# Attention and two feed-forward layers on one core: the weight rounding split into four planned operations, and two thirds of the key sums added before the matrix product

## The chip, the cores and the metric

One core of a Trainium2 chip runs the whole program. The metric is device time in microseconds from launch to the end. TensorE is called PE below, its weight loads PEld, VectorE DVE, ScalarE ACT, GpSimd POOL; SP's queue issues the DMAs.

## The reference, cut to what matters

Attention with exponential features, then a feed-forward layer with a leaky unit, then four gated experts:

```python
def phi(x):                                   # x: (4, 8, 576, 64), w_phi: (64, 128)
    proj = np.einsum('bhsd,df->bhsf', x, w_phi)
    proj = proj - np.max(np.abs(proj), axis=-1, keepdims=True)
    return np.concatenate([np.exp(proj), np.exp(-proj)], axis=-1)
q_p, k_p = phi(q), phi(k)
kv = np.einsum('bhsf,bhsd->bhfd', k_p, v)
z = np.sum(k_p, axis=2)                       # the key sums
num = np.einsum('bhsf,bhfd->bhsd', q_p, kv)
den = np.einsum('bhsf,bhf->bhs', q_p, z)[..., None] + 1e-06
attn = num / den
...
h = x @ w_in                                  # x: (2304, 512), w_in: (512, 2048)
x = (np.maximum(h, 0) + alpha * np.minimum(h, 0)) @ w_out
...
out = sum(p[:, e:e+1] * (np.maximum(x @ w1[e], 0) @ w2[e]) for e in range(4))
```

## The kernel before, in words

**Attention** takes two heads at a time: 16 pairs, numbered 0 to 15. The 576 keys of a pair are five tiles (four of 128, one of 64), handled as three units: tiles 0 and 1, tiles 2 and 3, tile 4. For a unit, PE projects keys (`Pk`, lines 339 to 341, three fp32r products a tile) into a PSUM tile `bank`; DVE takes the largest magnitude (line 346) and subtracts it (line 353, into `pmk`); ACT takes the two exponentials (line 359, into `ke`, a ring of two buffers); PE multiplies with the values (`KV`, line 370, two heads in two column halves) and, with a block of ones as the stationary operand, adds the keys up (line 376, 32 columns wide, in four column groups). Both land in the PSUM tile `kv`, of which there is one. Two ACT copies bring it to SBUF (`kvs`), PE turns it (lines 390 and 392), ACT copies it to `kvt`. Queries are projected and reduced alike (`pmq`), transposed on PE (line 411), exponentiated on ACT (line 418, `qe`) and multiplied with `kvt` (line 428); ACT and DVE copy numerator and denominator out of PSUM; DVE inverts the denominator in four instructions (lines 440 to 443); POOL, ACT and DVE form the result and split it into two fp32r parts `Xh` and `Xl`.

**Beside it** run two kinds of work that do not belong to a pair. Eight float64 weight blocks of the first feed-forward layer are rounded to fp32: a DMA, one ACT instruction (line 529), four DVE instructions with integer and float operations in the function `words` (lines 185 to 188), an add (line 533, DVE or POOL), and the split into two fp32r parts. And products of that layer for the first three blocks of 512 tokens: `U` (line 222, 12 matmuls into `mm`, a ring of two PSUM tiles), its leaky unit on DVE and ACT (lines 556 to 561, tiles `t`, `gh`, `gl`), and `M` (line 243, four chunks of 12 matmuls, which needs `gh` and `gl` of all four `U`), which ACT copies to `acc_a`. That is 24 groups of 12 matmuls.

**The order** of all this is made by a planner in the kernel, the class `Plan`: each operation has a cost by engine, predecessors, a rank, ring buffers that it allocates and reads. The planner repeatedly takes the operation that can begin first (ties by rank), on the engine that suits it, and writes its instructions; every engine then executes its own in that order. An operation is never interrupted by another on the same engine. `words` is one operation of four instructions here.

**After attention** the rest of the first layer (chunks of weights rounded the same way by `rounded`, lines 190 to 195) and the expert layer (lines 794 and 841) follow, in an order that the framework makes.

Of the kernel before, what the change touches and what calls it, by code (L numbers as in the profile page):

```python
# [11 lines left out]
F32 = mybir.dt.float32  # L12
F32R = mybir.dt.float32r
U32 = mybir.dt.uint32
AF = mybir.ActivationFunctionType
ALU = mybir.AluOpType
# [3 lines left out]
P = 128  # L20
B, H, S, D, F = 4, 8, 576, 64, 128
NP = H // 2
NT = B * S
DM = H * D
CC = DM // P
DFF = 2048
E, DE = 4, 1024
# [3 lines left out]
BLK = 512  # L31
# [3 lines left out]
UNITS = [(0, 1), (2, 3), (4,)]  # L35
# [8 lines left out]
EP = NF2 // 2  # L44
SEQ = (1, 5, 6, 2, 7, 3, 4)
NA = 3
AHEAD = 2


RANK = dict(  # L50
    ld=6.41, sp=11.67, Pk=-7.81, Pq=-3.81, E=11.17, Z=-20.34, KV=-7.89, TV=-14.97, Q=-17.39, A=-0.59, F=2.88,
    W=22.69, U=16.42, G=5.73,
)
WSTEP = 0.46
# [4 lines left out]
class Plan:  # L59
# [11 lines left out]
    def op(self, name, costs, after, rank, emit, alloc=(), reads=(), behind=(), late=0):  # L71
        self.ops[name] = (costs, after, rank, emit, alloc, {*after, *behind}, late)
        for x in reads:
            self.readers.setdefault(x, []).append(name)
# [63 lines left out]
def fused(ctx: ExitStack, tc: tile.TileContext, qT, kT, v_main, v_tail, w_phi, alpha, probs, w64, wup, wdn, out):  # L138
    nc = tc.nc
    pool = lambda name, bufs, stack=ctx, **k: stack.enter_context(tc.tile_pool(name=name, bufs=bufs, **k))  # L140
    f32 = lambda ap: ap.bitcast(F32)
# [21 lines left out]
    acc = [big.tile([P, CC, NA * BLK], F32, name="acc_a")]  # L163
# [17 lines left out]
    wts = {}  # L181
    raw = {}

    def words(r, u, lo, hi):
        nc.vector.tensor_scalar(r, r, 3, None, ALU.logical_shift_left)
        nc.vector.scalar_tensor_tensor(r, hi, 1 << 31, r, ALU.bitwise_and, ALU.bitwise_or)  # L186
        nc.vector.tensor_scalar(u, r, 0xFF800000, None, ALU.bitwise_and)
        nc.vector.scalar_tensor_tensor(f32(u), lo, 2.0**-52, f32(u), ALU.mult, ALU.mult)

    def rounded(w, r, u):  # L190

# [76 lines left out]
    with ExitStack() as st1:  # L268
# [8 lines left out]
        for args in (  # L277
            ("kr", 1, F32, P, S), ("qr", 1, F32, P, S), ("v", 1, F32, P, len(TILES), 2, D),
            ("kh", 1, F32R, P, S), ("kl", 1, F32R, P, S), ("qh", 1, F32R, P, S), ("ql", 1, F32R, P, S),
            ("m", 13, F32, P, 4), ("pmk", 2, F32, P, 4, F), ("pmq", 3, F32, P, 4, F), ("ke", 2, F32, P, 4, 2, F),  # L280
            ("kvs", 1, F32, P, 4, F), ("qe", 4, F32, P, 2, HMAX), ("kvt", 4, F32, P, 4, P),
            ("den", 2, F32, P, S), ("dt", 1, F32, P, S), ("num", 2, F32, P, S), ("di", 3, F32, P, S // 32, 1),
            ("gh", 5, F32R, P, BLK), ("gl", 5, F32R, P, BLK), ("t", 2, F32, P, BLK),
        ):
            ring(*args)
        ring("bank", 5, F32, P, 512, space=PSUM)
# [1 line left out]
        ring("mm", 2, F32, P, BLK, space=PSUM)  # L288
        ones = pool("ones", 1, st1).tile([P, 32], F32, name="ones")
        one = const.tile([P, 1], F32, name="one")  # L290
        busy = pool("busy", 1, st1).tile([P, 2 * F], F32, name="busy")
        tl = {}

        def new(name, key, dtype=None):
            p_, shape, dt = rings[name]
            tl[name, key] = p_.tile(shape, dtype or dt, name=name)
            return tl[name, key]

        engines = {"a": nc.scalar, "v": nc.vector, "p": nc.gpsimd}
        pe = lambda n, k=1: k * (n / 2.4 + 3)  # L300
        act = lambda n: 100 + 0.83 * n
        actp = lambda n: 52 + 0.83 * n
        dve = lambda n: 70 + 1.04 * n
        dve2 = lambda n: 70 + 0.52 * n
# [4 lines left out]
        op = plan.op  # L309
# [53 lines left out]
        def key_values(p, u):  # L363

            unit = UNITS[u]
            rows, e, v = TILES[unit[0]][1], flat(tl["ke", (p, u)]), tl["v", p]
            kv = new("kv", p) if u == 0 else tl["kv", p]
            for i, tile_ in enumerate(unit):
                for h in range(2):
                    nc.tensor.matmul(  # L370
                        kv[h * D:(h + 1) * D, 0], v[:rows, tile_, h], e[:rows, 2 * i + h],
                        start=tile_ == 0, stop=tile_ == len(TILES) - 1, skip_group_check=True)
            for i, tile_ in enumerate(unit):
                for h in range(2):
                    r = 32 * (2 * (tile_ % 2) + h)
                    nc.tensor.matmul(  # L376
                        kv[r:r + 32, 1], ones[:rows], e[:rows, 2 * i + h],
                        start=False, stop=tile_ + 2 >= len(TILES), tile_position=(0, r), skip_group_check=True)

        def save_kv(p, k, e):  # L380
            kvs = (new if k == 0 else lambda *x: tl[x])("kvs", p).rearrange("p (k s) f -> p k (s f)", k=2)
# [75 lines left out]
        for p in range(len(pairs)):  # L457
# [16 lines left out]
                op(("E", p, u), {"a": 2 * act(N_U[u])}, [("S", "k", p, u)], RANK["E"] + p + 0.1 * u, alloc=[("ke", (p, u))],  # L474
                   reads=[("pmk", (p, u))], emit=lambda e, a=(p, u): exp_keys(*a))
            for u in range(3):
                op(("KV", p, u), {"t": 595 * len(UNITS[u])}, [("E", p, u), ("ld", "v", p)] + [("KV", p, u - 1)] * (u > 0),
                   RANK["KV"] + p + 0.1 * u, alloc=[("kv", p)] if u == 0 else [], reads=[("ke", (p, u)), ("v", p)],
                   emit=lambda e, a=(p, u): key_values(*a))
            for k in range(2):  # L480
                op(("CV", p, k), copy_cost(256), [("KV", p, 2)], RANK["TV"] + p, alloc=[("kvs", p)] if k == 0 else [],
                   behind=[("CV", p, 0)] * k, reads=[("kv", p)], emit=lambda e, a=(p, k): save_kv(*a, e))
            op(("TV", p), {"t": 340}, [("CV", p, 0), ("CV", p, 1)], RANK["TV"] + p, alloc=[("bank", ("kv", p)), ("kvt", p)],
               reads=[("kvs", p)], emit=lambda e, p=p: turn_kv(p))
# [37 lines left out]
        def w_step(i, k, e):  # L522
            c, half = early[i]
            st64, w, u = areas[i % 2]
            lo, hi = st64[:, :, 0::2], st64[:, :, 1::2]
            if k == 0:
                nc.sync.dma_start(st64, w64[c, half].rearrange("p (a b) -> p a b", a=2))
            elif k == 1:
                nc.scalar.mul(f32(w), f32(hi), 2.0**-112)
            elif k == 2:  # L530
                words(w, u, lo, hi)
            elif k == 3:
                engines[e].tensor_tensor(f32(w), f32(w), f32(u), ALU.add)
            elif k == 4:
                for r, n in ((wa[half], "h"), (wa[half], "l")):
                    tl["w" + n, (c, half)] = r.tile([P, DM], F32R, name="w" + n + "ud"[half])
                cp(engines[e], tl["wh", (c, half)].rearrange("p (a b) -> p a b", a=2), f32(w))
            else:
                h, l = (tl["w" + n, (c, half)].rearrange("p (a b) -> p a b", a=2) for n in "hl")
                engines[e].tensor_tensor(l, f32(w), f32(h), ALU.subtract)  # L540
                wts[c, half] = tl["wh", (c, half)], tl["wl", (c, half)]

        for i, (c, half) in enumerate(early):
            costs = ({"d": 1500}, {"a": act(DM)}, {"v": 2 * dve2(DM) + 2 * dve(DM) + 330}, lo_cost(DM), hi_cost(DM), lo_cost(DM))
            for k, cost in enumerate(costs):
                op(("W", k, c, half), cost, [("W", k - 1, c, half)] * (k > 0), RANK["W"] + WSTEP * i,
                   alloc=[("area", i)] * (k == 0), reads=[("area", i)] * (k == 5), late=4200 * (k == 0),
                   emit=lambda e, i=i, k=k: w_step(i, k, e))


        def g_step(c, blk, k, e):
# [381 lines left out]
```

## Time and profile before

| | us |
|---|---|
| median of three runs | 1405.55 (1403.22 to 1406.3) |
| the profiled execution, its own time | 1402.89 |
| its span | 1401.0 |
| PE busy | 1380.2 |
| DVE / ACT / POOL busy | 774.2 / 509.5 / 272.8 |

The span is what the profiler saw; 1.9 us lie around it. PE is busy for all but 20.8 us of it. Attention ends at about 279 us, where the products of the last pair end; the three early blocks of the first layer end at about 323 us.

### The profile page before, as it was taken

How to read it: one execution, taken by the hardware profiler on the slowest of the kernel's cores; microseconds unless marked ns; L12 is line 12 of the kernel's file. 1: busy time of each engine (PE TensorE's matmuls, PEld its weight loads, DVE VectorE, ACT ScalarE, POOL GpSimd, SP SyncE). 2: the span in 40 equal slices, each digit the busy share in tenths (PEclk: the TensorE clock that was granted, in tenths of full speed). 3: DMA queues.
4: the chain of work that ended last, by engine and by line, in shares of the span. 5: the costliest groups of instructions: out<-in, count | busy, mean ns of one | idle time of the engine just before them, and what ended most of it. 6: DMA issues, size and time to landing. Idle time of an engine off the chain costs nothing.

```text
span 1401.0 us, 19675 instructions
## 1 busy us (share of the span) xinstructions
PE 1380.2 (99%) x7304; PEld 1167.4 (83%) x7304; DVE 774.2 (55%) x1292; ACT 509.5 (36%) x1112; POOL 272.8 (19%) x276
## 2 busy tenths in 40 slices
PE   8999999989999999999999999999999999999998
PEld 5667766668888888889889898999899889988997
DVE  7876655587967956575544454633333363333343
ACT  6876666632212212124434443322122232221220
POOL 3443322221201104006655562000000000000000
PEclk9999999999999999999999999999999999999999
DMA  4311111032200202005886776665556667655541
GB/s 155 112 52 52 52 51 52 10 105 61 90 16 20 71 1 90 31 0 211 314 294 226 245 254 222 207 228 189 166 171 192 191 205 229 197 184 165 174 157 45
DMA packets 102208, 192.25 MB, mean 137 GB/s; under 512 B 11617, under 2 KB 12769, under 8 KB 102113
## 3 DMA queue, kind: packets, MB, share of 16 engines
q1 hardware_dynamic: 102112, 191.00, 42.2%
q8 instruction: 58, 0.95, 0.3%
q14 instruction: 38, 0.30, 0.1%
HBM read 140.10 MB, written 50.86 MB: 136 GB/s over the span
## 4 chain that ended last, share of the span: by engine, by line
PE 91%; DVE 4%; ACT 2%; DMA 2%; POOL 1%; issue 0%; SPq 0%; POOLq 0%; DVEq 0%
PE dn L841 28%; PE up L794 24%; PE up L222 12%; PE dn L243 12%; PE bank L428 4%; PE kv L370 2%; PE mm L243 2%; PE mm L222 2%; PE kv L376 2%; PE bank L411 1%; PE bank L339 1%; PE bank L341 1%; PE bank L340 1%; DMA acc_a<-w 0%; DVE acc_a L186 0%
## 5 line engine op out<-in xcount | busy, mean ns | idle before, releaser
L841 PE MATMUL dn<-whd,Xh 128*128 128x512 f32 x720 | 231.4, 390 | 0.0
L852 DVE SCALAR_TENSOR_TENSOR acc<-dn,pr,acc 128x512 f32<-128x512 f32 x126 | 88.7, 750 | 190.9 <-PE dn L841 190.9
L794 PE MATMUL up<-Xl,wlu 128*128 128x384 f32 x864 | 158.8, 335 | 1.0 <-DVE c L807 0.5
L841 PEld LDWEIGHTS dn<-whd,Xh 128*128 128x128 f32 x720 | 135.2, 188 | 27.0
L794 PEld LDWEIGHTS up<-Xl,wlu 128*128 128x128 f32 x864 | 150.3, 188 | 2.3 <-DVE c L807 1.4
L841 PE MATMUL dn<-Xh 128*128 128x512 f32 x648 | 151.8, 389 | 0.0
L807 DVE TENSOR_TENSOR c<-up,p 128x384 f32<-128x384 f32 x96 | 53.5, 558 | 174.7 <-PE up L794 172.0
L841 PEld LDWEIGHTS dn<-Xh 128*128 128x128 f32 x648 | 121.7, 188 | 25.5
L812 ACT COPY p<-up 128x384 f32<-128x384 f32 x48 | 23.0, 480 | 326.1 <-PE up L794 326.1
L841 PE MATMUL dn<-wld,Xh 128*128 128x512 f32 x360 | 140.8, 391 | 0.0
L794 PE MATMUL up<-Xl,whu 128*128 128x384 f32 x576 | 112.0, 334 | 0.8 <-ACT p L812 0.7
L801 ACT ACTIVATE Xh<-c 128x384 fp32r<-128x384 f32 x144 | 75.7, 526 | 79.3 <-DVE c L807 79.3
L794 PEld LDWEIGHTS up<-Xl,whu 128*128 128x128 f32 x576 | 101.2, 188 | 1.4 <-ACT p L812 1.4
L222 PE MATMUL up<-Xl,whu 128*128 128x512 f32 (+1 forms) x272 | 99.1, 364 | 0.0
L222 PE MATMUL up<-Xh,whu 128*128 128x512 f32 (+1 forms) x272 | 99.1, 364 | 0.0
L243 PE MATMUL dn<-gh,wld 128*128 128x512 f32 (+1 forms) x272 | 99.1, 364 | 0.0
L243 PE MATMUL dn<-gh,whd 128*128 128x512 f32 (+1 forms) x272 | 99.1, 364 | 0.0
L222 PE MATMUL up<-Xh,wlu 128*128 128x512 f32 (+1 forms) x272 | 99.0, 364 | 0.0
L243 PE MATMUL dn<-gl,whd 128*128 128x512 f32 (+1 forms) x272 | 99.0, 364 | 0.0
L175 ACT CAST gh<-t 128x512 fp32r<-128x512 f32 (+1 forms) x68 | 38.6, 568 | 149.5 <-DVE t L234 149.5
L802 DVE SCALAR_TENSOR_TENSOR Xh<-c,Xh 128x384 fp32r<-128x384 f32 x144 | 85.5, 595 | 5.5
L841 PEld LDWEIGHTS dn<-wld,Xh 128*128 128x128 f32 x360 | 67.5, 188 | 13.0
(166 smaller groups left out, 2481.7 us busy)
## 6 DMA issues: line engine op xcount, KB each, us to landing
whu<-wsu SPq DMA_DIRECT2D x96, 256.0 KB, 3.5
wlu<-wsu SPq DMA_DIRECT2D x96, 256.0 KB, 3.2
st<-w SPq DMA_DIRECT2D x24, 512.0 KB, 3.6
wsu<-whu SPq DMA_DIRECT2D x48, 256.0 KB, 3.1
wsu<-wlu SPq DMA_DIRECT2D x48, 256.0 KB, 2.6
Xh<-wsd SPq DMA_DIRECT2D x48, 256.0 KB, 3.8
wld<-wsd SPq DMA_DIRECT2D x40, 256.0 KB, 3.1
whd<-wsd SPq DMA_DIRECT2D x40, 256.0 KB, 3.6
```

The costliest lines, as they stand in the source:

```text
L175: nc.scalar.copy(hi, src)
L222: nc.tensor.matmul(ps[:, :bn], a[:, cs], x[:, cc, t0:t0 + bn], start=n == 0, stop=n == 3 * CC - 1)
L243: nc.tensor.matmul(ps, w[:, sl], g, start=start and k == 0, stop=stop and k == 2)
L370: nc.tensor.matmul(kv[h * D:(h + 1) * D, 0], v[:rows, tile_, h], e[:rows, 2 * i + h], start=tile_ == 0, stop=tile_ == len(TILES) - 1, skip ...
L376: nc.tensor.matmul(kv[r:r + 32, 1], ones[:rows], e[:rows, 2 * i + h], start=False, stop=tile_ + 2 >= len(TILES), tile_position=(0, r), ski ...
L428: nc.tensor.matmul(nd[:, :n], tl["kvt", p][:, 2 * h + s], tl["qe", (p, h, c)][:, s, :n], start=s == 0, stop=s == 1)
L794: nc.tensor.matmul(ps[name], w[k][:, r, kt * P:(kt + 1) * P], slots[k][:, x + kt], start=start and n == 0, stop=stop and n == 5, skip_grou ...
L801: nc.scalar.activation(gh, src, AF.Relu)
L802: nc.vector.scalar_tensor_tensor(gl, src, 0.0, f32(gh), ALU.max, ALU.subtract)
L807: nc.vector.tensor_tensor(o, ps[name], x, ALU.add)
L841: nc.tensor.matmul(ps[m], x[:, sl], w, start=c == chunks[0] and k == 0, stop=c == chunks[-1] and k == 2)
L852: nc.vector.scalar_tensor_tensor(av, ps[m], pe, av, ALU.mult, ALU.add)
```

## The change

It does four things.

1. The four instructions of `words` become four operations of the planner (`W` steps 2, 2.25, 2.5, 2.75), so that it may place other DVE work between them. The instructions are the same.
2. From the sixth pair on (`NZ = 5`, pairs 5 to 15) the products with ones of the first two units are left out. Instead the exponentials of unit 0 and unit 1 are added on DVE or POOL into a new tile `zsum` of 128x1024 (operation `Z`), and one batch of four products with ones multiplies that sum, after the third unit (operation `ZZ`). The second copy of `kv` to SBUF waits for `ZZ`.
3. To make room for `zsum`, the rings `gh` and `gl` of this stage have four buffers instead of five, and the tile `busy` of the first four warming matmuls lies in `acc_a`.
4. The planner's cost of `KV` falls for the first two units of those pairs. With that, its order changes on every engine up to the end of the stage.

```diff
-    def words(r, u, lo, hi):
-        nc.vector.tensor_scalar(r, r, 3, None, ALU.logical_shift_left)
-        nc.vector.scalar_tensor_tensor(r, hi, 1 << 31, r, ALU.bitwise_and, ALU.bitwise_or)
-        nc.vector.tensor_scalar(u, r, 0xFF800000, None, ALU.bitwise_and)
-        nc.vector.scalar_tensor_tensor(f32(u), lo, 2.0**-52, f32(u), ALU.mult, ALU.mult)
+    def word(n, r, u, lo, hi):
+        if n == 0:
+            nc.vector.tensor_scalar(r, r, 3, None, ALU.logical_shift_left)
+        elif n == 1:
+            nc.vector.scalar_tensor_tensor(r, hi, 1 << 31, r, ALU.bitwise_and, ALU.bitwise_or)
...
+    def words(*a):
+        for n in range(4):
+            word(n, *a)
...
-            ("gh", 5, F32R, P, BLK), ("gl", 5, F32R, P, BLK), ("t", 2, F32, P, BLK),
+            ("zsum", 1, F32, P, 4, 2 * F), ("gh", 4, F32R, P, BLK), ("gl", 4, F32R, P, BLK), ("t", 2, F32, P, BLK),
...
-        busy = pool("busy", 1, st1).tile([P, 2 * F], F32, name="busy")
+        busy = acc[0][:, 1, :2 * F]
...
+            if p >= NZ and u < 2:
+                return
             for i, tile_ in enumerate(unit):
                 for h in range(2):
                     r = 32 * (2 * (tile_ % 2) + h)
...
+        def sum_keys(p, e):
+            engines[e].tensor_tensor(new("zsum", p), flat(tl["ke", (p, 0)]), flat(tl["ke", (p, 1)]), ALU.add)
+
+        def add_up(p):
+            for m in range(4):
+                nc.tensor.matmul(tl["kv", p][32 * m:32 * m + 32, 1], ones, tl["zsum", p][:, m],
+                                 start=False, stop=True, tile_position=(0, 32 * m), skip_group_check=True)
...
-                op(("KV", p, u), {"t": 595 * len(UNITS[u])}, [("E", p, u), ("ld", "v", p)] + [("KV", p, u - 1)] * (u > 0),
+                op(("KV", p, u), {"t": (595 - 155 * (p >= NZ and u < 2)) * len(UNITS[u])}, [("E", p, u), ("ld", "v", p)] + [("KV", p, u - 1)] * (u > 0),
...
+            kv_sums = [("KV", p, 2)]
+            if p >= NZ:
+                op(("Z", p), lo_cost(1024), [("E", p, 0), ("E", p, 1)], RANK["Z"] + p, alloc=[("zsum", p)],
+                   reads=[("ke", (p, u)) for u in range(2)], emit=lambda e, p=p: sum_keys(p, e))
+                op(("ZZ", p), {"t": 310}, [("KV", p, 2), ("Z", p)], RANK["TV"] + p, reads=[("zsum", p)], emit=lambda e, p=p: add_up(p))
+                kv_sums = [("ZZ", p)]
             for k in range(2):
-                op(("CV", p, k), copy_cost(256), [("KV", p, 2)], RANK["TV"] + p, alloc=[("kvs", p)] if k == 0 else [],
+                op(("CV", p, k), copy_cost(256), kv_sums if k else [("KV", p, 2)], RANK["TV"] + p, alloc=[("kvs", p)] if k == 0 else [],
...
-            elif k == 2:
-                words(w, u, lo, hi)
+            elif 2 <= k < 3:
+                word(int(4 * (k - 2)), w, u, lo, hi)
...
-            costs = ({"d": 1500}, {"a": act(DM)}, {"v": 2 * dve2(DM) + 2 * dve(DM) + 330}, lo_cost(DM), hi_cost(DM), lo_cost(DM))
+            costs = {
+                0: {"d": 1500}, 1: {"a": act(DM)}, 2: {"v": dve2(DM)}, 2.25: {"v": dve(DM)}, 2.5: {"v": dve2(DM)}, 2.75: {"v": dve(DM)},
+                3: lo_cost(DM), 4: hi_cost(DM), 5: lo_cost(DM),
+            }
```

**PE, pair 8, from its first product with the values to its last product with ones.** `kv<-ke,v` are products with the values, `kv<-ke,ones` and `kv<-zsum,ones` the key sums, `bank<-wbh,kh` and the two behind it a projection, `bank<-qe,kvt` products with queries, `bank<-ident,pmq` transposes; x4 counts instructions. Before:

```order
L370 MATMUL kv<-ke,v 64x256 x4
L376 MATMUL kv<-ke,ones 32x256 x4
L339 MATMUL bank<-wbh,kh 64x256
L340 MATMUL bank<-wbl,kh 64x256
L341 MATMUL bank<-wbh,kl 64x256
L370 MATMUL kv<-ke,v 64x256 x4
L376 MATMUL kv<-ke,ones 32x256 x4
L428 MATMUL bank<-qe,kvt 128x256 x4
L411 MATMUL bank<-ident,pmq 128x128 x4
L370 MATMUL kv<-ke,v 64x256 x2
L376 MATMUL kv<-ke,ones 32x256 x2
```

Now, in the same pair (lines are those of the changed file):

```order
L379 MATMUL kv<-ke,v 64x256 x4
L430 MATMUL bank<-ident,pmq 128x128 x2
L379 MATMUL kv<-ke,v 64x256 x4
L348 MATMUL bank<-wbh,kh 64x256
...
L447 MATMUL bank<-qe,kvt 128x256 x2
L447 MATMUL bank<-qe,kvt 128x320 x2
L430 MATMUL bank<-ident,pmq 128x128 x4
L430 MATMUL bank<-ident,pmq 128x64
L379 MATMUL kv<-ke,v 64x256 x2
L387 MATMUL kv<-ke,ones 32x256 x2
L447 MATMUL bank<-qe,kvt 128x320 x2
L396 MATMUL kv<-zsum,ones 32x256 x4
```

Two batches of four products with ones are gone, one stands after the third unit, with two query products between.

**DVE, the weight instructions around the inversion of pair 1.** `acc_a<-acc_a` are the four instructions of `words`, `m<-bank` the largest magnitude, `pmk` and `pmq` the subtraction. Before, two whole roundings in a row stand ahead of the inversion (the transposes) and of the next pair's reductions:

```order
L185 TENSOR_SCALAR acc_a<-acc_a 128x512
L186 SCALAR_TENSOR_TENSOR acc_a<-acc_a 128x512
L187 TENSOR_SCALAR acc_a<-acc_a 128x512
L188 SCALAR_TENSOR_TENSOR acc_a<-acc_a 128x512
L185 TENSOR_SCALAR acc_a<-acc_a 128x512
L186 SCALAR_TENSOR_TENSOR acc_a<-acc_a 128x512
L187 TENSOR_SCALAR acc_a<-acc_a 128x512
L188 SCALAR_TENSOR_TENSOR acc_a<-acc_a 128x512
L440 STREAM_TRANSPOSE dt<-den 128x576
```

Now, at the corresponding place, the instructions stand one or two at a time between the reductions and subtractions of the last unit:

```order
L355 TENSOR_REDUCE m<-bank 64x2
L189 SCALAR_TENSOR_TENSOR acc_a<-acc_a 128x512
L362 TENSOR_TENSOR pmq<-bank,m 64x256
L191 TENSOR_SCALAR acc_a<-acc_a 128x512
L187 TENSOR_SCALAR acc_a<-acc_a 128x512
L193 SCALAR_TENSOR_TENSOR acc_a<-acc_a 128x512
L355 TENSOR_REDUCE m<-bank 64x2
L189 SCALAR_TENSOR_TENSOR acc_a<-acc_a 128x512
L362 TENSOR_TENSOR pmk<-bank,m 64x256
L325 TENSOR_TENSOR kl<-kr,kh 128x576
L191 TENSOR_SCALAR acc_a<-acc_a 128x512
L193 SCALAR_TENSOR_TENSOR acc_a<-acc_a 128x512
```

The same instructions as before, spread out, with an inversion behind them as before.

**DVE after the last pair's inversion.** `t<-mm` and `gl<-t` are the leaky unit of the early products `U`; `w<-w` and `w<-st,w` are the first rounding of the following stage, which waits for its data by DMA. Now (before, the rows from `t<-mm` on are the same, up to the second rounding):

```order
L462 STREAM_TRANSPOSE den<-di 128x576
L586 TENSOR_SCALAR t<-mm,alpha_sb 128x512
L587 SCALAR_TENSOR_TENSOR t<-mm,t 128x512
L591 TENSOR_TENSOR gl<-t,gh 128x512
L586 TENSOR_SCALAR t<-mm,alpha_sb 128x512
L587 SCALAR_TENSOR_TENSOR t<-mm,t 128x512
L187 TENSOR_SCALAR w<-w 128x512
L189 SCALAR_TENSOR_TENSOR w<-st,w 128x512
L591 TENSOR_TENSOR gl<-t,gh 128x512
L586 TENSOR_SCALAR t<-mm,alpha_sb 128x512
L191 TENSOR_SCALAR u<-w 128x512
L587 SCALAR_TENSOR_TENSOR t<-mm,t 128x512
```

What moved is on PE: before, 13 of the 24 groups of 12 early products stand behind the last pair's products (two `U`, four `M`, three `U`, four `M`); now eight do (four `U`, then four `M`), and 16 stand between the pairs. Of the 11 operations `Z`, eight stand on DVE and three on POOL.

## Rows read from the trace of the kernel before

**Rows 1.** The page: busy time of each engine, its share of the span, instructions.

```profile
PE 1380.2 (99%) x7304; PEld 1167.4 (83%) x7304; DVE 774.2 (55%) x1292; ACT 509.5 (36%) x1112; POOL 272.8 (19%) x276
```

**Rows 2.** Four stretches: length, busy PE, PEld, DVE, ACT, POOL (instructions), clock, DMA.

```profile
10.00:100.00 90.00, 81.89 (x572) 53.18 (x572) 73.37 (x127) 71.29 (x173) 39.45 (x29) 1.00 0.33 101
100.00:278.00 178.00, 178.00 (x1166) 125.61 (x1167) 105.88 (x198) 120.93 (x297) 50.51 (x36) 1.00 0.15 43
278.00:307.00 29.00, 24.74 (x105) 19.14 (x104) 22.57 (x37) 11.85 (x22) 7.20 (x5) 1.00 0.34 108
307.00:1401.00 1094.00, 1088.48 (x5433) 965.23 (x5432) 567.81 (x927) 301.12 (x615) 174.33 (x197) 1.00 0.48 156
```

**Rows 3.** Waits of PE up to 330 us: waiter <- releaser: total, times, longest.

```profile
PE kv L370 <- ACT ke L359: 5.0, 6, 1.6
...
PE bank L428 <- DVE pmk L353: 2.1, 3, 0.9
...
PE bank L341 <- POOL kl L316: 0.9, 1, 0.9
PE bank L339 <- DVE pmk L353: 0.7, 1, 0.7
```

**Rows 4.** Chain that ended last, pair 6: start, us, instruction (x2 records a matmul).

```profile
106.18 1.01 PE kv L370 x8
107.20 0.57 PE kv L376 x8
107.77 0.26 PE bank L339
...
108.26 1.01 PE kv L370 x8
109.28 0.57 PE kv L376 x8
...
111.77 0.44 PE bank L411 x4
```

**Rows 5.** DVE in order of time, the same pair: start, duration, what it waited for.

```profile
108.30 0.42 DVE L346 TENSOR_REDUCE m<-bank 64x2 f32<-64x256 f32 x1 [0.47 <-PE bank L341]
...
110.57 0.41 DVE L353 TENSOR_TENSOR pmq<-bank,m 64x256 f32<-64x256 f32 x1
...
117.42 0.78 DVE L440 STREAM_TRANSPOSE dt<-den 128x576 f32<-128x576 f32 x1 [4.79 <-ACT den L143]
```

**Rows 6.** Groups up to 330 us, POOL: | busy us, mean ns | idle before, releaser.

```profile
L454 POOL TENSOR_TENSOR Xl<-num,Xh 128x576 fp32r<-128x576 f32 x15 | 21.5, 1430 | 10.5 <-ACT Xh L143 10.5
L561 POOL TENSOR_TENSOR gl<-t,gh 128x512 fp32r<-128x512 f32 x5 | 6.4, 1279 | 3.8 <-ACT gh L143 3.8
```

**Rows 7.** DVE, PE and POOL in order of time, at 18 and at 51 to 57 us.

```profile
18.51 1.65 DVE L186 SCALAR_TENSOR_TENSOR acc_a<-acc_a 128x512 uint32<-128x512 uint32 x1
...
51.09 0.69 DVE L188 SCALAR_TENSOR_TENSOR acc_a<-acc_a 128x512 f32<-128x512 uint32 x1
...
56.21 1.97 PE L428 MATMUL bank<-qe,kvt 128*128 128x256 f32 x8 [0.93 <-DVE pmk L353]
...
18.16 1.46 POOL L540 TENSOR_TENSOR wlu<-acc_a,whu 128x512 fp32r<-128x512 f32 x1
```

**Rows 8.** PE and DVE after the last pair; ACT's wait for the DMA.

```profile
278.68 0.64 PE L222 MATMUL mm<-Xh,whu 128*128 128x512 f32 x1
...
284.40 0.39 PE L243 MATMUL mm<-gh,whd 128*128 128x512 f32 x1
...
306.01 0.50 PE L222 MATMUL mm<-Xh,whu 128*128 128x512 f32 x1 [2.34 <-DVE t L557]
...
284.96 0.75 DVE L556 TENSOR_SCALAR t<-mm,alpha_sb 128x512 f32<-128x512 f32 x1
...
289.02 0.43 DVE L185 TENSOR_SCALAR w<-w 128x512 uint32<-128x512 uint32 x1 [2.58 <-ACT w L193]
...
288.31 0.67 ACT L193 ACTIVATE w<-st 128x512 f32<-128x512 f32 x1 [3.42 <-DMA st<-w]
```

More of the change, by code (lines that the diff above doesn't have):

```diff
@@ L46 @@
 NA = 3
+NZ = 5
 AHEAD = 2
@@ L182, in fused @@
     raw = {}
-    def words(r, u, lo, hi):
-        nc.vector.tensor_scalar(r, r, 3, None, ALU.logical_shift_left)
-        nc.vector.scalar_tensor_tensor(r, hi, 1 << 31, r, ALU.bitwise_and, ALU.bitwise_or)
-        nc.vector.tensor_scalar(u, r, 0xFF800000, None, ALU.bitwise_and)
-        nc.vector.scalar_tensor_tensor(f32(u), lo, 2.0**-52, f32(u), ALU.mult, ALU.mult)
+    def word(n, r, u, lo, hi):
[3 more added lines that the diff above has]
+            nc.vector.scalar_tensor_tensor(r, hi, 1 << 31, r, ALU.bitwise_and, ALU.bitwise_or)
+        elif n == 2:
+            nc.vector.tensor_scalar(u, r, 0xFF800000, None, ALU.bitwise_and)
+        else:
+            nc.vector.scalar_tensor_tensor(f32(u), lo, 2.0**-52, f32(u), ALU.mult, ALU.mult)
+    def words(*a):
+        for n in range(4):
+            word(n, *a)
     def rounded(w, r, u):
@@ L543, in fused @@
         for i, (c, half) in enumerate(early):
-            costs = ({"d": 1500}, {"a": act(DM)}, {"v": 2 * dve2(DM) + 2 * dve(DM) + 330}, lo_cost(DM), hi_cost(DM), lo_cost(DM))
-            for k, cost in enumerate(costs):
-                op(("W", k, c, half), cost, [("W", k - 1, c, half)] * (k > 0), RANK["W"] + WSTEP * i,
+            costs = {
+                0: {"d": 1500}, 1: {"a": act(DM)}, 2: {"v": dve2(DM)}, 2.25: {"v": dve(DM)}, 2.5: {"v": dve2(DM)}, 2.75: {"v": dve(DM)},
+                3: lo_cost(DM), 4: hi_cost(DM), 5: lo_cost(DM),
+            }
+            before = []
+            for k, cost in costs.items():
+                op(("W", k, c, half), cost, before, RANK["W"] + WSTEP * i,
                    alloc=[("area", i)] * (k == 0), reads=[("area", i)] * (k == 5), late=4200 * (k == 0),
                    emit=lambda e, i=i, k=k: w_step(i, k, e))
+                before = [("W", k, c, half)]
         def g_step(c, blk, k, e):
```

## The prediction

> **What bounds the kernel now.** I read the busy times first: PE works for 1380.2 of 1401.0 us [rows 1], and the granted clock is 1.00, the upper level of 2.4 GHz, in every stretch [rows 2]. So the end is set by PE's work and by PE's gaps, 20.8 us in all. Then I read where the gaps lie [rows 2]: 8.1 us between 10 and 100, none between 100 and 278, 4.3 us between 278 and 307, and 5.5 us after that, where the change touches nothing; what is left, 2.9 us, is the start. The stretch from 100 to 278 us is the one to look at longest: DVE works there for 59% and ACT for 68% of the time, and PE never waits. Whatever leaves PE's queue there shortens the program; whatever is added to DVE there is free until PE starts to wait for it. In the first 100 us it is the other way round: between 10 and 100 DVE works for 73.4 of 90 us and PE waits for what DVE makes, directly (2.1 and 0.7 us on `pmk`) or through the exponentials of ACT (5.0 us), and 0.9 us for POOL [rows 3].
>
> **The key sums on PE.** The chain gives the price of a batch by the distance of the starts: four products with ones take 0.57 us, and so do those of the second unit [rows 4]. That is one switch and four column groups that run together, since the four products with values, on two column groups, take 1.01 us [rows 4]. A pair from the sixth on loses two such batches and gains one, which has the same four instructions, the same 256 columns and the same column groups: 0.57 - 2 * 0.57 = -0.57 us. For 11 pairs that is **-6.3 us**. The first row behind a batch is 0.26 us long where its like takes about 0.12 [rows 4], so a change of tile shape costs some 0.14 us. If a removed batch left its switch behind, it would save only 0.43 us, and a pair 0.29 us: -3.2 us is the poor end. I take -6.3, because every batch in the chain, of values too, carries a switch of its own, and a batch that is not there has none.
>
> **The addition on DVE or POOL.** The trace has no 1024-wide addition. The nearest rows are 512 wide: on DVE an instruction with two such inputs takes 0.69 us [rows 7], on POOL 1.28 us, and 1.43 us for 576 columns [rows 6]. Going on by that slope (0.15 us for 64 columns) POOL needs about 2.5 us; DVE, at twice its own 512, at most 1.4 us and, with one start for both halves, about 1.25. These are estimates. Eight on DVE come to 10 us, three on POOL to 7.5 us. In the middle stretch DVE has room: within pair 6 it waits 0.47 us for PE before the last unit's reduction, and 4.79 us for ACT's copies before the inversion [rows 5]. The sum stands in the first of these places, ahead of the last unit's reductions, so it hides 0.47 us and delays what follows by about 0.8. Who waits for that: the transpose of the second head's queries, whose PSUM buffer comes free when the last subtraction (`pmq`) is done. Before, that subtraction ends at 110.98 us and the transposes begin at 111.77 [rows 4, 5]: 0.8 us to spare. Now PE comes there 1.14 us earlier, since two batches are gone, while the projection that DVE needs comes 0.57 us earlier. So the delay of 0.8 and the missing 0.57 eat the 0.8 us and leave PE some 0.5 us late, if nothing else gives. Eight pairs at 0.5 us are 4 us at worst, and zero if the order is looser, as in the pairs where two transposes stand before the second product with values. I take **+1.5 us**. The lower bound is zero, since nothing in this step removes a wait of PE.
>
> The new wait of the second `kvs` copy, for `ZZ`, lies on ACT; behind it stand exponentials of the queries. Query products or transposes lie between the batch and the turning of `kv` on PE in every pair, and hide the copy, so I cost it at nothing; uncovered it would be, for 256 columns, less than the 0.67 us that ACT takes for 512 [rows 8], at most 7.4 us in 11 pairs.
>
> **The weight instructions.** Nothing is added or removed: the same 32 instructions, about 18 us of DVE, stand in finer pieces. What can be won is the part of the 8.1 us that PE waits behind a whole block of them. One such place: two blocks end on DVE at 51.78 us [rows 7], the inversion and the next pair's reductions come late, and the query products wait 0.93 us for `pmk` at 56.21 [rows 7]. By the order of DVE I put the 2.8 us of waits for `pmk` and two of the six waits for `ke`, some 1.6 of 5.0 us [rows 3], down to such blocks, and the 0.9 us for POOL to an addition of a weight that stood ahead of `kl` and now stands behind it: 5.3 us. But DVE stays busy for four fifths of this stretch, and sums and early products (the first comes about one pair sooner) join in, so I take two thirds: **-3.5 us**. The ends are zero, and -8 for all gaps.
>
> **Fewer early products at the end, fewer buffers.** Five groups of 12 move from behind the last pair to between the pairs. PE does them in either place, so by itself this is nothing. Behind the last pair PE waited 4.3 us [rows 2], the longest 2.34 us for DVE's leaky unit [rows 8], which stood among roundings of the next stage. Now four `U` run there from the end of the query products. Two took 5.72 us (278.68 to 284.40 [rows 8]), so four take 11.4, and the first `M` needs the PSUM buffer of the third `U`. On DVE that unit stands behind the first rounding, which waits for ACT, and ACT for a DMA: in the trace the rounding begins 10.3 us after the query products end (278.68 to 289.02 [rows 8]). Two of its instructions, the subtraction `gl`, and the two instructions of the leaky unit with one more rounding instruction between take 0.43 + 0.69 + 0.69 + 0.75 + 0.43 + 0.69 = 3.7 us [rows 7, 8]: +14.0. PE waits 2.6 us instead of 4.3: **-1.7 us**, between -4.3 (no wait) and +1.5. The fourth buffer of `gh` and `gl` is enough for these groups, since each block uses four and its `M` are all done before the next block begins; a fifth would let one `U` of the next block go ahead, as it did once before. The roundings of the next stage now start nearer to their use, by about 14 us of PE's work (five groups at 2.86); they are used after the early blocks' end at 323 us and a whole further block, so I cost that at nothing; if it fails, the wait would show after 307 us.
>
> **Sum.** -6.3 + 1.5 - 3.5 - 1.7 = -10.0 us against the profiled execution's 1402.9: 1392.9 us. That execution lies 2.7 us under the median of the runs, so against the median of 1405.55 the forecast is **1395.5 us**.
>
> **The rivals.** *More than that:* all gaps up to 100 us but the start close (-8), the end waits 2 us less than I say, and the sums delay nothing: -6.3 - 8 - 3.7 = -18.0, **1387.5 us**. For it: the planner has 16 groups to fill between pairs instead of 11. Against it: DVE's load before 100 us is the same.
>
> *Absorbed:* PE's gain in the middle turns into waits for the vector engines. Every pair's transposes wait 0.5 us, and the weight pieces win nothing: -6.3 + 4 - 1.7 + 0 = -4.0, and with the switch left behind (-3.2 for -6.3) -0.9: 1401.5 to 1404.6, about **1403 us**. For it: the 0.8 us of slack above. Against it: the 4.8 us for which DVE stands idle in each pair.
>
> What two engines do to each other bears on this. A DVE instruction with two SBUF inputs took 1.65 us instead of 0.69 when it began beside a POOL instruction that ended at 19.62 us [rows 7]. The Trainium skill, "SBUF — State Buffer", section "SBUF: two separate sides", says that such a DVE operation and a POOL operation share a port pair as an exclusive lock, so that the later one blocks fully. By that rule the trace agrees: the DVE instruction ended 0.54 us after POOL's. As a mechanism here, all eight sums on DVE would run into a POOL addition and lose 0.96 us each, the difference in the rows: 7.7 us more on DVE, directly ahead of the subtraction that PE needs. Were none of it hidden, 1395.5 + 7.7 = 1403.2 us, the same place as the absorbed case; I give it 0.04 of that case's 0.13, since the 4.8 us of idle DVE time in a pair can take it up.
>
> *Slower:* the exponentials of the third unit write the `ke` buffer of the first, which the sum reads too. So ACT waits for the sum, with its other exponentials and copies queued behind it, and PE for ACT. Where the sum is late, behind two POOL additions of 1.43 us, or on DVE behind four subtractions, PE loses perhaps 1.4 us a pair, 15.4 us in 11 pairs in place of 1.5: -10.0 - 1.5 + 15.4 = +3.9, **1409.5 us**. It decides from about 1.05 us a pair (11.5 / 11), where the gain is gone. Against it: the sum may start when the second unit's exponentials end, and the third unit's product with values comes 6 us after the first's (106.18 to 112.21, where the transposes end [rows 4]).
>
> **How the numbers follow.** Forecast 0.57, more 0.22, absorbed 0.13, slower 0.08. A difference under 0.2% (2.8 us) can hardly be told from none in this kernel. The forecast and its better rival are both faster, and a few hundredths of the absorbed case: 0.82; within 0.2%: 0.11; slower: 0.07. The range leaves out the last of the better rival and most of the slow one: 1386 to 1404.5.
>
> **What would show it.** Right: PE's work up to the end of the early blocks falls by about 6 us in its key-sum batches (22 fewer, 11 new, 0.57 us each); no gap over 0.5 us before a transpose between 100 us and the last pair; fewer PE waits on `pmk` and `ke` before 100 us; one wait of 2 to 3 us behind the last pair's early `U`. Wrong: waits of PE for `pmq`, `kvs` or `ke` in every pair from the sixth on, or a wait for the new sum itself; batches of sums longer than 0.57 us; or a new gap after 307 us, which would mean that the later roundings lost their lead.

## The result and the profile after

The changed kernel takes 1391.18 us (median of five runs, 1389.41 to 1392.42) beside 1405.09 us for the kernel before in the same comparison: ratio 0.9904, 95% interval 0.989 to 0.9917. It is faster by 13.9 us, about 1%; a gain of 10.0 us had been forecast. The profiled execution has a span of 1389.4 us, 11.6 less than the 1401.0 of before.

The busy line of the page after, as in [rows 1]:

```profile
PE 1375.0 (99%) x7216; PEld 1166.5 (84%) x7216; DVE 779.9 (56%) x1298; ACT 510.4 (37%) x1115; POOL 283.1 (20%) x278
```

PE works 5.2 us less, so 6.4 of the 11.6 us are idle time that went. The four stretches after, with the columns of [rows 2]:

```profile
10.00:100.00 90.00, 86.41 (x594) 58.83 (x595) 80.53 (x141) 73.27 (x176) 34.49 (x25) 0.98 0.35 101
100.00:278.00 178.00, 178.00 (x1098) 125.58 (x1097) 106.07 (x192) 120.12 (x297) 64.35 (x43) 1.00 0.16 43
278.00:307.00 29.00, 26.73 (x115) 21.07 (x114) 21.45 (x37) 11.88 (x23) 5.78 (x4) 1.00 0.24 73
307.00:1389.40 1082.40, 1076.52 (x5384) 956.63 (x5382) 567.29 (x924) 300.90 (x614) 177.20 (x198) 1.00 0.48 158
```

Length less busy PE is the idle time: 3.6 us instead of 8.1 between 10 and 100 us, none from 100 to 278 as before, 2.3 instead of 4.3 behind the last pair, 5.9 instead of 5.5 after that. And the granted clock of the first stretch is 0.98, not 1.00. Before 100 us other waits of PE are left than in [rows 3] (total, times, longest, up to 330 us):

```profile
PE bank L430 <- DVE pmq L362: 2.4, 2, 1.4
PE mm L252 <- DVE t L587: 1.7, 1, 1.7
PE kv L379 <- ACT ke L368: 1.3, 2, 1.1
...
PE mm L252 <- DVE gl L591: 0.6, 1, 0.6
PE bank L447 <- DVE pmk L362: 0.5, 1, 0.5
```

The six waits for `ke` (5.0 us) are two (1.3), the four for `pmk` (2.8) one (0.5), the one for POOL is gone. New are two waits for `pmq` (2.4), which end at 13.17 and 17.40 us. The waits behind `t` and `gl` are those behind the last pair.

### The profile page after: what moved, and what is told of

Read it like the earlier page. It is cut to its first block, busy times and chain, and to the rows that moved or that the text cites. A ratio compares the mean times of both kernels' runs of the same rounds, so it can differ in the third digit from the quotient of the medians.

```text
span 1389.4 us, 19497 instructions
## 1 busy us (share of the span) xinstructions
PE 1375.0 (99%) x7216; PEld 1166.5 (84%) x7216; DVE 779.9 (56%) x1298; ACT 510.4 (37%) x1115; POOL 283.1 (20%) x278
## 4 chain that ended last, share of the span: by engine, by line
PE 94%; DMA 2%; DVE 2%; ACT 1%; issue 0%; SPq 0%; POOL 0%; POOLq 0%; DVEq 0%; ACTq 0%
PE dn L871 28%; PE up L824 24%; PE up L231 12%; PE dn L252 12%; PE bank L447 4%; PE kv L379 3%; PE mm L252 2%; PE bank L348 2%; PE mm L231 2%; PE bank L430 2%; PE bank L349 1%; PE bank L350 1%; PE kv L387 1%; DMA w<-wdn 1%; PE kv L396 0%; DMA acc_a<-w 0%
```

## The experiments

Times are medians; differences are to the changed kernel's 1391.18 us where nothing else is said. The kernel before was timed again beside each group of runs, with medians from 1403.38 to 1405.09 us, so a difference of 1 to 2 us between groups can't be told by the times alone; there the traces have to decide.

### The order alone: no sums

```diff
-            if p >= NZ and u < 2:
-                return
...
-            engines[e].tensor_tensor(new("zsum", p), flat(tl["ke", (p, 0)]), flat(tl["ke", (p, 1)]), ALU.add)
+            pass
```

(`add_up` is left empty too; the planner still counts both operations, so the order stays.)

> The plan of the changed kernel with its order on every engine, but from the sixth pair on the sums of keys are made as before: TensorE multiplies every unit of keys by the ones, and the addition and its product are left out. The output is the same. Theory (the key sums are work that TensorE itself loses, 22 batches of 0.57 us less and 11 of 0.57 more): 6.3 us more than the changed kernel, 1397.5 us (1396.5 to 1398.5), TensorE's busy time 1381.3 instead of 1375.0, and the idle time before 100 us as in the changed kernel. Rival (the gain is the new order, and the products of keys would lie beside something else): at most 1 us more, 1391.2 to 1392.2.

Measured: 1395.33 us (1393.86 to 1396.22), 4.2 more: under the theory's range and over the rival's. The two traces have the same order up to the last pair, so the price of the key sums can be read pair by pair, from the start of the products that turn `kv`. First the changed kernel, pairs 4 (the last without the sum) and 15, then the same rows here (start, duration):

```profile
79.25 0.56 PE L411 MATMUL bank<-sel,kvs 128*128 128x64 f32 x4
276.04 0.56 PE L411 MATMUL bank<-sel,kvs 128*128 128x64 f32 x4
```

```profile
79.47 0.56 PE L407 MATMUL bank<-sel,kvs 128*128 128x64 f32 x4
281.34 0.56 PE L407 MATMUL bank<-sel,kvs 128*128 128x64 f32 x4
```

201.87 us here, 196.79 in the changed kernel: 5.08 us for 11 pairs, 0.46 a pair, where 0.57 had been worked out. Taken pair by pair it is 0.38 to 0.49 in seven and 0.54 to 0.55 in four. Of these 5.1 us the changed kernel gives back 0.9, of which 0.5 behind the last pair (it waits 1.7 and 0.6 us there, this one 1.2 and 0.6) and the rest in the later layers.

### The product of the sum beside the other product with ones

```diff
+            if p >= NZ:
+                add_up(p)          # at the end of key_values, u == 2
...
-                   ... reads=[("zsum", p)], emit=lambda e, p=p: add_up(p))
+                   ... reads=[("zsum", p)], emit=lambda e: None)
```

> The changed kernel with the product of each pair's sum moved on TensorE to right behind the last unit's own sum of keys, instead of behind a product of queries; the planner's order of all else is kept. Theory (a pair saves 0.40 us instead of 0.57 where the product of the sum stands between a product of queries and a transpose, 0.55 where it doesn't: it is the change of the tiles' shape on TensorE, twice, that eats the rest): 0.15 us less in each of some six pairs, about 0.9 us less, 1390.3 us (1389.3 to 1391.3), and the step from one pair to the next shorter by that in the trace. Rival (the sums come late, so that the earlier place turns into a wait for VectorE or GpSimd): more than 1392 us and a wait for the sum.

Measured: 1389.32 us (1388.44 to 1390.53), ratio to the kernel before 0.9895 (0.9881 to 0.9908). Where the lost part of a pair lies is seen in pair 6, PE in order of time, first in the changed kernel:

```profile
112.67 1.34 PE L447 MATMUL bank<-qe,kvt 128*128 128x320 f32 x4
113.94 0.64 PE L396 MATMUL kv<-zsum,ones 128*32 128x256 f32 x8
114.51 0.64 PE L430 MATMUL bank<-ident,pmq 128*128 128x128 f32 x3
115.08 1.34 PE L447 MATMUL bank<-qe,kvt 128*128 128x320 f32 x4
```

and then with the product moved:

```profile
112.06 0.62 PE L387 MATMUL kv<-ke,ones 64*32 64x256 f32 x4
112.61 0.64 PE L398 MATMUL kv<-zsum,ones 128*32 128x256 f32 x8
113.18 1.34 PE L449 MATMUL bank<-qe,kvt 128*128 128x320 f32 x4
114.36 0.58 PE L432 MATMUL bank<-ident,pmq 128*128 128x128 f32 x3
114.88 1.34 PE L449 MATMUL bank<-qe,kvt 128*128 128x320 f32 x4
```

From the start of the query products to the start behind the transposes: 2.41 us (112.67 to 115.08) above; below, where the sum stands ahead of them, 1.70 (113.18 to 114.88). So the batch costs 0.71 us between query products and transposes and 0.57 (112.61 to 113.18) beside the other batch with ones, whose tiles have 64 rows (64*32 instead of 128*32). From pair 4 to pair 15 the kernel with the moved product needs 195.67 us:

```profile
79.41 0.56 PE L413 MATMUL bank<-sel,kvs 128*128 128x64 f32 x4
275.08 0.56 PE L413 MATMUL bank<-sel,kvs 128*128 128x64 f32 x4
```

That is 6.2 us less than without sums, the forecast's 6.3, and no wait for the sum appeared. By the times alone this kernel can't be told from the changed one (the intervals overlap); by the trace it is 1.1 us better.

The gain lies in seven pairs (0.08 to 0.21 us each). In the other four, 10 and 13 to 15, it is 0.02 to 0.03 us, though there too the sum stood between others in the changed kernel, behind the transposes. Pair 10 in the changed kernel, and its transposes by tile shape:

```profile
183.46 0.62 PE L387 MATMUL kv<-ke,ones 64*32 64x256 f32 x4
184.01 0.64 PE L430 MATMUL bank<-ident,pmq 128*128 128x128 f32 x3
184.60 0.64 PE L396 MATMUL kv<-zsum,ones 128*32 128x256 f32 x8
185.17 1.34 PE L447 MATMUL bank<-qe,kvt 128*128 128x320 f32 x4
```

```profile
L430 PE MATMUL bank<-ident,pmq x3: 272/272/332, 184.0 to 184.4; 128*128 128x128 f32 x2, 64*128 64x64 f32 x1
```

The last transpose is on 64*128, so the shape changes ahead of the query products whether the sum stands there or not: from the last unit's ones to the query products there are four changes in either place. In pair 6 and the six like it the move takes one change away. So the theory of the tile shape holds in all eleven pairs, with one change saved and not the two that it named; being away from the other ones costs nothing by itself.

### The addition done twice

```diff
+            engines[e].tensor_tensor(tl["zsum", p], flat(tl["ke", (p, 0)]), flat(tl["ke", (p, 1)]), ALU.add)
```

> The changed kernel, but each of the 11 additions of two units of keys is done twice on its engine (the same addition into the same buffer, 1.24 us more on VectorE in eight pairs, 2.38 us more on GpSimd in three); TensorE's order is the same. Theory (the additions lie beside TensorE's work, which has time enough before it needs the sum): 1391 to 1392 us, no wait of TensorE for the sum of over 0.5 us. Rival (the additions are part of the path, so that the forecast's 1.5 us of delay is paid and the doubled ones pay it again and more): 8 x 1.24 = 10 us more, 1399 to 1401 us.

Measured: 1390.83 us (1390.14 to 1391.04), no difference, and from pair 5 to pair 15 every pair's step agrees with the changed kernel's to 0.01 us (the step from pair 4 to pair 5 is 0.23 longer). The additions lie beside PE. In the changed kernel they took (count; least, median, most ns):

```profile
L392 DVE TENSOR_TENSOR zsum<-ke x8: 1214/1241/1596, 88.6 to 266.7; 128x1024 f32<-128x1024 f32 x8
L392 POOL TENSOR_TENSOR zsum<-ke x3: 2377/2381/2384, 104.6 to 214.1; 128x1024 f32<-128x1024 f32 x3
```

### The rounding whole again

```diff
-            elif 2 <= k < 3:
-                word(int(4 * (k - 2)), w, u, lo, hi)
+            elif k == 2:
+                words(w, u, lo, hi)
...
-                0: {"d": 1500}, 1: {"a": act(DM)}, 2: {"v": dve2(DM)}, 2.25: {"v": dve(DM)}, 2.5: {"v": dve2(DM)}, 2.75: {"v": dve(DM)},
+                0: {"d": 1500}, 1: {"a": act(DM)}, 2: {"v": 2 * dve2(DM) + 2 * dve(DM) + 330},
```

> The changed kernel with the rounding of a weight as one operation of the planner again; the sums of keys as in the changed kernel. Theory (the split is what shortened TensorE's idle time between 10 and 100 us from 8.1 to 3.6 us, and it also brought the drop of the clock at 18.7 us, which costs about 1.7 us): the idle time there is about 8 us again and the clock 1.00 throughout, so 4.5 - 1.7 = 2.8 us more than the changed kernel, 1394.0 us (1392.5 to 1395.5). Rival (the split is worth nothing, and the idle time fell because the added sums took the place of other work): 1391 us or less.

Measured: 1395.17 us (1394.69 to 1396.42), 4.0 more, in the theory's range. Two stretches and two waits of PE in this kernel:

```profile
10.00:100.00 90.00, 81.15 (x556) 53.02 (x560) 75.33 (x129) 69.88 (x169) 39.56 (x29) 1.00 0.33 102
...
278.00:307.00 29.00, 27.45 (x117) 21.36 (x116) 19.98 (x33) 12.01 (x23) 2.97 (x2) 1.00 0.24 73
```

```profile
PE kv L379 <- ACT ke L368: 5.5, 6, 1.6
PE bank L447 <- DVE pmk L362: 2.2, 3, 1.0
```

The six waits for `ke` and the three for `pmk` are back, almost as in [rows 3], and the idle time between 10 and 100 us is 8.9 us. So it is the split that closes these gaps. The 1.6 us behind the last pair, against 4.3 in [rows 2], don't need it.

### The split alone

```diff
-NZ = 5
+NZ = 16
```

> The changed kernel with no sums of keys (the old products in all 16 pairs), but the rounding of a weight as four operations. Theory (the two parts stand beside each other): the split alone is worth the 4.5 us of idle time before 100 us less 1.7 us of the lower clock, and the key sums the rest, so 1391.2 + 6.3 = 1397.5 us, and up to 2 us more if the last products of the stage wait as in the kernel before: 1397 to 1399.5. Rival (the split is what gives nearly all of it, through the whole stage): below 1395 us. Rival (the split gives nothing without the sums): 1404 to 1406 us.

Measured: 1396.24 us (1394.82 to 1397.25): 0.8 us under the theory's range, over the 1395 us of the first rival and far under the 1404 of the second. Two stretches:

```profile
10.00:100.00 90.00, 85.36 (x597) 57.40 (x598) 78.98 (x140) 73.31 (x177) 36.59 (x27) 1.00 0.33 101
...
278.00:307.00 29.00, 26.79 (x109) 21.39 (x109) 24.36 (x39) 9.94 (x18) 4.37 (x3) 0.94 0.34 109
```

By the spans (1395.5 and 1389.4) it is 6.1 more: the 5.1 us of the sums, as read from the kernel with the order alone, and 1.1 us more idle time before 100 us. So the two parts stand beside each other, and the theory's figure was too large by the same misjudged 6.3. Of the 8.1 us of idle time before 100 us the split closes 3.5 without the sums. It is worth about 8.4 us against the 1404.62 us of the kernel before in that comparison, the sums without the split (the kernel above) 9.5. That is 17.9 us, 4.0 more than both at once (13.9). By the spans, with 1.3 us taken off for the stretch at the lower clock (see the last experiment), it is 6.8 and 7.6 us, together 14.4 against 13.6, so most of the 4.0 lies in the scatter of the medians. The end of the stage is shorter in either kernel (2.2 and 1.6 us idle instead of 4.3) and is counted twice in such a sum.

### The smaller rings alone

```diff
-            ("gh", 5, F32R, P, BLK), ("gl", 5, F32R, P, BLK), ("t", 2, F32, P, BLK),
+            ("gh", 4, F32R, P, BLK), ("gl", 4, F32R, P, BLK), ("t", 2, F32, P, BLK),
```

> The kernel before with four instead of five buffers for each of the two halves of the activations, nothing else. Theory (the buffers that the sum displaced cost or give nothing until the last pair, where only the order of the last products changes): within 2 us of the kernel before, 1403 to 1407 us, idle time up to 278 us as before. Rival (the smaller ring by itself is the better end of the stage): 1402 us or less.

Measured: 1403.8 us (1400.76 to 1405.33), ratio to the kernel before 0.9992 (0.9983 to 1.0001). The buffers are worth nothing that can be told.

### The next stage's staging area on early-freed buffers

```diff
-            ("kr", 1, F32, P, S), ("qr", 1, F32, P, S), ("v", 1, F32, P, len(TILES), 2, D),
+            ("qe", 4, F32, P, 2, HMAX), ("kvt", 4, F32, P, 4, P), ("den", 2, F32, P, S), ...
...
+            ("kr", 1, F32, P, S), ("qr", 1, F32, P, S),
```

> The changed kernel with its buffers of this stage declared in another order, so that the staging area of the next stage's weights lies on the loaded keys and queries, which come free early, and not on the last pair's denominators. Nothing else is changed. Theory (the 1.71 us that TensorE waits at 296.49 hang on the chain denominators, transfer, VectorE's steps on the weight, products' activation): the transfer starts some us earlier, the wait behind the last pair shrinks by 1.5 to 2.3 us, 1388.9 to 1389.7 us. Rival (the wait hangs on VectorE's queue itself, whichever step stands in it): no change, 1390.5 to 1392 us.

Measured: 1390.43 us (1389.4 to 1391.55), between the theory's range and the rival's, next to the rival's. The waits decide for the rival. The data did come earlier. The first step of the rounding, first in the changed kernel, then here:

```profile
292.93 0.43 DVE L187 TENSOR_SCALAR w<-w 128x512 uint32<-128x512 uint32 x1 [2.03 <-ACT w L202]
```

```profile
286.96 0.99 DVE L187 TENSOR_SCALAR w<-w 128x512 uint32<-128x512 uint32 x2 [0.72 <-ACT w L202]
```

But PE now waits 1.24 us for `t` ahead of the fourth `U` and 1.0 us for `gl` in two places, 2.2 us in all, much the same as the 2.3 in the changed kernel:

```profile
PE mm L231 <- DVE t L588: 1.2, 1, 1.2
...
PE mm L252 <- DVE gl L592: 1.0, 2, 0.5
```

DVE has the leaky units and the rounding to do in either case; the earlier rounding only changed which step came late. The run does not show the earlier data alone, because DVE's order behind the last pair changed with it: two first steps of the rounding now stand ahead of the first `gl`.

### The first block of weights planned later

```diff
-                   alloc=[("area", i)] * (k == 0), reads=[("area", i)] * (k == 5), late=4200 * (k == 0),
+                   alloc=[("area", i)] * (k == 0), reads=[("area", i)] * (k == 5), late=(9000 if i == 0 else 4200) * (k == 0),
```

> The changed kernel with the planner told that the first block of weights arrives 9.0 us after its request instead of 4.2 us; the order of the first 100 us changes, the end of the stage does not. Theory (the waits of TensorE at 13.17 and 17.40 us, 2.4 us together, come from the difference of queries standing behind the first step of a rounding whose data comes later than planned, and the lower clock from 18.7 to 22.7 us is what follows them in some executions): the two waits are gone, the clock is 1.00, so 2 to 4 us less than the changed kernel, 1387.2 to 1389.2 us. Rival (what waits there is behind the exponentials and the maxima anyway): less than 1 us less, 1390.2 or more.

Measured: 1392.56 us (1392.16 to 1394.1), 1.4 more, on the rival's side. The two waits for `pmq` are gone and the first pair is 4.8 us shorter, but the gain is given back by pair 6, whose products that turn `kv` start at 118.50 us instead of 116.48: 5.4 us idle between 10 and 100 us, and five waits for `ke`. The longest, on PE, and what ACT did ahead of it:

```profile
38.52 1.62 PE L379 MATMUL kv<-ke,v 128*64 128x256 f32 x8 [1.72 <-ACT ke L368]
```

```profile
36.19 0.66 ACT L554 ACTIVATE acc_a<-acc_a 128x512 f32<-128x512 f32 x1 [2.38 <-DMA acc_a<-w]
36.76 0.65 ACT L144 CAST Xh<-num 128x576 fp32r<-128x576 f32 x1
37.32 2.19 ACT L368 ACTIVATE ke<-pmk 128x512 f32<-128x512 f32 x4
```

The exponentials stand behind a weight whose data isn't there, now on ACT. The theory was right on what the two waits hang on and wrong on what comes late next. It was wrong on the clock too: that fell all the same, to 0.50 between 40 and 42 us, behind the wait of 1.72 us shown above, so it does not hang on the two waits for `pmq`.

### Sums in all pairs, and from the fourth on

```diff
-NZ = 5
+NZ = 0        # and 3 in the other
```

Both with the product of the sum beside the other product with ones.

> The changed kernel with the sum's product beside the last unit's own sum of keys, and the two units of keys added in all 16 pairs instead of from the sixth on; the planner orders the first 100 us anew for it. Theory (in the first five pairs TensorE is not what is waited for throughout: 3.6 us idle between 10 and 100 us, behind VectorE and ScalarE, which the additions load further): of 5 x 0.57 = 2.85 us saved on TensorE at least half comes back as waits before 100 us, 1388.5 to 1391 us, that is no clear gain over the same kernel with sums from the sixth pair (1389.3). Rival (TensorE is the bound there too): 2.5 us less than that, 1387 us or less.

> The same with the sums from the fourth pair on. Theory (as above): 2 x 0.57 = 1.1 us saved on TensorE, of which waits before 100 us take back a part: 1388 to 1390 us. Rival (TensorE is the bound there too): 1388 us or less, with no more idle time between 10 and 100 us than the 3.6 us of the changed kernel.

Measured: 1390.93 us (1387.83 to 1391.2) and 1390.80 us (1390.17 to 1394.22): no gain on the 1389.32 us with sums from the sixth pair. The second is 0.8 us beyond its range. The idle time between 10 and 100 us is 6.5 and 6.3 us instead of 3.6; the row for all pairs, with a lower clock in two places:

```profile
10.00:100.00 90.00, 83.53 (x534) 56.48 (x535) 80.36 (x132) 70.42 (x173) 43.80 (x29) 0.96 0.34 99
```

In the first five pairs PE's saved work turns into waits; there the vector engines set the pace.

### The changed kernel once more

Nothing is edited.

> The changed kernel itself once more, as the measure for the two beside it and for the run with the sum's product moved: 1390 to 1392 us if the earlier 1391.2 us holds; the lower clock between 18 and 23 us may be there or not (theory: it comes in some executions of the same order, and is worth 1.5 us).

Measured: 1389.94 us (1389.24 to 1393.56). Its profiled execution has a span of 1387.4 us, 2.0 less than the earlier one of the same kernel. Two stretches of 2 us (columns as in [rows 2]), first the earlier execution, then this one:

```profile
18.00:20.00 2.00, 2.00 (x12) 1.04 (x12) 1.97 (x4) 1.62 (x6) 0.71 (x1) 0.79 0.39 108
20.00:22.00 2.00, 2.00 (x11) 2.00 (x11) 1.83 (x2) 0.78 (x2) 1.27 (x2) 0.50 0.78 218
```

```profile
18.00:20.00 2.00, 2.00 (x16) 1.18 (x16) 1.97 (x4) 1.63 (x6) 0.86 (x1) 1.00 0.53 132
20.00:22.00 2.00, 2.00 (x20) 2.00 (x19) 2.00 (x3) 1.13 (x3) 1.27 (x2) 1.00 0.42 143
```

PE is busy throughout in both, but at a granted clock of 0.50, the lower level of 1.2 GHz, it gets 11 instructions done in 2 us instead of 20. From the second pair to the last the earlier execution is 1.42 to 1.45 us behind at the products that turn `kv`. 0.15 us of that were there before the clock fell (the transposes at 17.40 us start at 17.25 here), so one such stretch costs about 1.3 us. The four stretches of this execution, as in [rows 2]:

```profile
10.00:100.00 90.00, 86.43 (x603) 58.74 (x604) 81.75 (x143) 74.04 (x178) 36.19 (x26) 1.00 0.35 102
100.00:278.00 178.00, 178.00 (x1093) 125.31 (x1092) 105.94 (x191) 119.87 (x296) 63.00 (x42) 1.00 0.15 43
278.00:307.00 29.00, 26.93 (x115) 21.18 (x114) 21.69 (x39) 12.88 (x25) 5.78 (x4) 1.00 0.26 75
307.00:1387.40 1080.40, 1075.00 (x5377) 954.91 (x5375) 565.41 (x921) 299.77 (x613) 176.16 (x198) 1.00 0.48 159
```

## Why the prediction was right, and where it was off

The sign, the range and three of the four terms held in kind; the forecast was 4.3 us too high, and the better rival (1387.5) was 3.7 too low, so the time lies nearer to that rival. To compare the terms I set the kernel before, whose profiled execution had the upper clock throughout [rows 2], against the second execution of the changed one (span 1387.4 us, PE busy 1374.2, upper clock throughout): -13.6 us, beside -13.9 by the medians.

- **The key sums:** forecast -6.3, measured -5.1. The step that went wrong is the price of the new batch. That a removed batch takes its switch with it is right; but the new one was to cost 0.57 us wherever it stands, and in seven pairs its place added a change of tile shape, so that it cost 0.71 in the pair shown. With the change saved the total is -6.2. The poor end (-3.2) put the loss at the wrong place, on the removed batches.
- **The addition's delay:** forecast +1.5, measured 0. The prices were right: 1.24 us on DVE (estimate 1.25), 2.38 on POOL (2.5). What failed is the order that I took over from before: in the pair at 177 us DVE's last subtraction ends at 180.15 us, 1.1 us before the transposes, because eight query products (179.44 to 181.27) now stand ahead of them. PE waits for nothing between 100 us and the last pair. A POOL instruction beside the addition does cost: of the eight additions on DVE four began with POOL idle and took 1.21 or 1.22 us, three began 0.2 us before a POOL instruction ended and took 1.26 to 1.28, and one began 0.51 us before the end of one and took 1.60:

```profile
87.82 1.30 POOL L565 TENSOR_TENSOR wld<-acc_a,whd 128x512 fp32r<-128x512 f32 x1
88.61 1.60 DVE L392 TENSOR_TENSOR zsum<-ke 128x1024 f32<-128x1024 f32 x1 [0.83 <-ACT ke L368]
```

The Trainium skill ("SBUF — State Buffer", section "SBUF: two separate sides") says that a DVE instruction with two SBUF inputs and a POOL instruction that reads SBUF share a port pair as an exclusive lock, so that the later one blocks. These rows agree with that nearly: the addition ended 1.09 us after POOL's instruction, 0.13 less than it takes alone. The rival that let all eight additions run into POOL did not come about, because only one of them began well before a POOL instruction ended.
- **The weight pieces:** forecast -3.5, measured -4.5 (8.1 to 3.6 us of idle time), and -3.5 with the split alone. The term was made of two misses that partly cancel: the waits for `ke`, `pmk` and POOL fell by 6.9 us in the first execution, more than the 5.3 that I had put down to whole blocks, and 2.4 us of new waits for `pmq` came, which the forecast had not counted; the third taken off had to cover them.
- **The end of the stage:** forecast -1.7 with 2.6 us of waiting left, measured -2.2 with 2.1 left, 2.3 in the first execution. The longest single wait is 1.5 to 1.7 us, and it comes where it was expected, behind the four `U`, by the steps of DVE that were added up; the rounding began 9.4 us after the query products (283.49 to 292.93), not 10.3. The second wait, 0.5 us for `gl`, was not in the sum. And the rounding's wait for its data does not set the total alone: with the staging area moved the rounding began 5.4 us after the query products, and 2.2 us of waiting were left, with another order on DVE.
- **Costed at nothing:** the later roundings and the buffers, rightly (5.4 us idle after 307 us, as in [rows 2] but for 0.1). Not in the sum at all: 1.7 us by which PE's work after the first 10 us fell beyond the sums (1373.1 us by [rows 2], 1366.4 in the second execution, 5.1 of the 6.7 being the sums). What these 1.7 are was not tried alone; the kernel with the order alone has PE busy for 1372.8 us after the first 10, with one stretch at the lower clock, so about 1371.5 without, which is 1.6 less than before with the same products. The new order thus has them, and fewer changes of tile shape would fit, but this is argued only.

The sum of the terms on equal clocks is -5.1 + 0 - 4.5 - 2.2 = -11.8, with 1.7 for the last point -13.5. The absorbed rival fell with the doubled addition, the slower one with the absence of any wait for `ke` from the sixth pair on. The better rival was right on the delay and nearer than the forecast on the gaps, but the gaps did not all close, and it had the key sums at -6.3 too.

## What to carry to other kernels

Ask of each stretch which engine sets its pace: the same added sums were worth the work they take from PE where PE never waits, and nothing in the first five pairs, where it does. Price a small batch on PE with its neighbours, by the changes of tile shape that its place adds: where it added one more it cost 0.71 us here, else 0.57. And where a long piece of low urgency stands in an engine's queue, cutting it lets the urgent work through; moving its data earlier or later only moved the wait here.

## What the runs showed of the hardware that was not expected

The clock can fall for a few microseconds in one execution and not in the next of the same kernel and order. In the first execution of the changed kernel it fell to 0.50 at about 19.2 us, after waits of PE of 1.07, 1.43 and 0.95 us (ending at 10.09, 13.17 and 17.40 us), and rose again at about 22.6 us with PE busy. In the second the waits were 1.06, 1.15 and 0.95 us and it stayed at 1.00. But with the addition done twice they were 1.07, 1.47 and 0.95 us, and with the split alone 1.07, 1.73 and 0.95, and it stayed at 1.00 there as well. A lower clock came behind single waits too: in the split alone (0.94 between 278 and 307 us) behind one of 2.21 us that ended at 295.48, yet not behind the 2.34 us at 306.01 in the kernel before [rows 8]. So the length of the waits alone does not decide it, and what does is open. At about 1.3 us a time it is as large as some terms of the sum, so one profiled execution is not enough to judge such a term by its span.
